# Own PSUM tiles for a weight product, spread copies and a re-cut last tile in a fused attention and maxout kernel

**Chip, cores, metric.** One core of one Trainium2 chip. The metric is the device time of one execution in microseconds, the median of several runs. All ratios are of fast runs: a run over 1.5% above the fastest of its kernel counts as slow and is left out.

## The reference

Block attention with a Sinkhorn-normalised block permutation, then a maxout MLP without bias. Cut to what matters here:

```python
# q, k, v: (4, 8, 768, 64); sort_net: (4, 8, 8, 8)
P = sinkhorn(sort_net, 5 rounds)
k_sorted, v_sorted = P applied to the 8 blocks of k and v
attn = softmax(q_b @ k_sb.T / 8) @ v_sb            # per block of 96
x = attn_out as (3072, 512)
h1, h2 = x @ w1, x @ w2                            # (3072, 1024)
return np.maximum(h1, h2) @ w_out                  # (3072, 512), float32
```

The kernel uses max(h1, h2) = relu(h1 - h2) + h2, so out = relu(x (W1 - W2)) Wout + x (W2 Wout). It computes W2 Wout (512 x 512, "wc") once: 32 transposes of W2, then four groups of eight matmuls. That work stands in the first of four batches, between its attention and its output products.

## The kernel before

All PSUM tiles come from one pool of four buffers of two banks each. TensorE's program is hand-ordered: `units` are the MLP steps of a batch, and attention steps of the next batch are put between them. The parts concerned (cuts marked with `# ...`):

```python
psum = ctx.enter_context(tc.tile_pool(name="psum", bufs=4, space=bass.MemoryType.PSUM))

def w2_transposes(t, eng):          # half t of W2: 16 transposes into one tile
    ps = ps_bf16("tw_ps")
    for n in range(16):
        # ... nc.tensor.matmul(ps[:, n*128:(n+1)*128], w2_sb[...], ident, is_transpose=True)
    def out():
        w = 2048 // len(eng)
        for n, e in enumerate(eng):  # "AD": first half on ScalarE, second on VectorE
            evac(w2T[...][:, n*w:(n+1)*w], ps[:, n*w:(n+1)*w], w, two_x=True, eng=e)
    return out

def w_product(dmt, eng=None):        # two products share a tile, one copy for both
    m = dmt % 2
    if m == 0:
        wc_ps[0] = ps_f32("wc_ps")
    for fb in range(NFB):
        nc.tensor.matmul(wc_ps[0][:, m*512:(m+1)*512], w2T[:, fb, ...], wo_sb[:, fb, :], ...)
    if m == 1:
        evac(wc[:, dmt-1:dmt+1, :]..., wc_ps[0], 1024, eng=eng)
# ...
# batch 0: v of the later batches is turned by 8 copies of 12 columns on VectorE
VA[1:6] = [(lambda f=f, g=g: (f(), g())) for f, g in zip(VA[1:6], tns)]
TR[0:2] = [(lambda f=f, g=g: (f(), g())) for f, g in zip(TR[0:2], tns[5:])]
SC[7:] = [lambda f=SC[7], g=tns[7]: (f(), g())]
# ...
steps[-1:] = group(VA[1], TR[0])     # a values step and an x transpose stand in one step
```

SC, VA and TR are scores, values and x-transpose steps. The last output tile of 128 tokens is cut by columns into pieces, each with its own PSUM tile, copy and store: `(0, 256, "A"), (256, 384, "D"), (384, 512, "A")`.

The softmax here doesn't subtract the row's maximum and nothing guards it: scores larger than these inputs give would overflow.

Of the kernel before, what the change touches and what calls it, by code (L numbers as in the profile page):

```python
# [15 lines left out]
def kernel(  # L16
# [16 lines left out]
    nc = tc.nc  # L33
# [4 lines left out]
    B, H, S, D = q.shape  # L38
# [26 lines left out]
    def ps_f32(name):  # L65
        return psum.tile([128, 1024], FP32, tag="ps", name=name)

    def ps_bf16(name):
        return psum.tile([128, 2048], BF16, tag="ps", name=name)
# [21 lines left out]
    def pick(a_ns, d_ns):  # L91
        if load["A"] + a_ns <= load["D"] + d_ns:
            load["A"] += a_ns
            return "A"
        load["D"] += d_ns
        return "D"

    def evac(out_ap, in_ap, n, two_x=False, eng=None):
        a_ns, d_ns = (200 + n) / 1.2, (130 + (n / 2 if two_x else n)) / 0.96
        if eng:  # L100
            load[eng] += a_ns if eng == "A" else d_ns
        if (eng or pick(a_ns, d_ns)) == "A":
            nc.scalar.copy(out=out_ap, in_=in_ap)  # L103
        else:
            nc.vector.tensor_copy(out=out_ap, in_=in_ap)  # L105
# [16 lines left out]
    for n in range(NE):  # L122
        t = big.tile([BLK, 8 * BLK + 32], BF16, tag=f"e{n}", name=f"e{n}")
# [35 lines left out]
    w2_sb = big.tile([128, HP, DFF], BF16, tag="w2", name="w2_sb")  # L159
# [16 lines left out]
    ident = const.tile([128, 128], BF16, tag="ident", name="ident")  # L176
# [345 lines left out]
    w2T = big.tile([128, NFB, DMODEL], BF16, tag="w2T", name="w2T")  # L522
    wc = big.tile([128, HP, DMODEL], BF16, tag="wc", name="wc")

    def w2_transposes(t, eng):
        ps = ps_bf16("tw_ps")
        for n in range(16):
            fb, dmt = t * 4 + n // 4, n % 4
            nc.tensor.matmul(  # L529
                ps[:, n * 128 : (n + 1) * 128],  # L530
                w2_sb[:, dmt, fb * 128 : (fb + 1) * 128],
                ident,
                is_transpose=True,
                start=True,
                stop=True,
            )
        def out():
            w = 2048 // len(eng)
            for n, e in enumerate(eng):
                evac(  # L540
                    w2T[:, t * 4 : t * 4 + 4, :].rearrange("p f d -> p (f d)")[
                        :, n * w : (n + 1) * w
                    ],
                    ps[:, n * w : (n + 1) * w],
                    w,
                    two_x=True,
                    eng=e,
                )

        return out  # L550

    wc_ps = {}

    def w_product(dmt, eng=None):
        m = dmt % 2
        if m == 0:
            wc_ps[0] = ps_f32("wc_ps")
        for fb in range(NFB):
            nc.tensor.matmul(  # L559
                wc_ps[0][:, m * 512 : (m + 1) * 512],  # L560
                w2T[:, fb, dmt * 128 : (dmt + 1) * 128],
                wo_sb[:, fb, :],
                start=(fb == 0),
                stop=(fb == NFB - 1),
            )
        if m == 1:
            evac(wc[:, dmt - 1 : dmt + 1, :].rearrange("p t n -> p (t n)"), wc_ps[0], 1024, eng=eng)


    g_tiles = {}  # L570
# [33 lines left out]
    def out_products(dst, b, ti, n0=0, n1=512, part=None):  # L604
        ch, off = divmod(ti * 128, TCH)
        for m in range(NFB + HP) if part is None else range(part * 6, part * 6 + 6):
            hp = m - NFB
            nc.tensor.matmul(  # L608
                dst,
                g_tiles[b, ch, m // 2][:, m % 2, off : off + 128]  # L610
                if m < NFB
                else xT[:, b % 2, ch, hp % 2, hp // 2, off : off + 128],
                wo_sb[:, m, n0:n1] if m < NFB else wc[:, hp, n0:n1],
                start=(m == 0),
                stop=(m == NFB + HP - 1),
            )
# [16 lines left out]
    def moe_out_last(ti, pieces):  # L633

        tok0 = (B - 1) * S + ti * 128
        for n0, n1, eng in pieces:
            ps = ps_f32("out_ps")
            out_products(ps[:, 0 : n1 - n0], B - 1, ti, n0, n1)
            o = opool.tile([128, n1 - n0], FP32, tag=f"o{ti}{n0}", name="o", bufs=1)
            if eng == "A":  # L640
                nc.scalar.copy(out=o, in_=ps[:, 0 : n1 - n0])
            else:
                nc.vector.tensor_copy(out=o, in_=ps[:, 0 : n1 - n0])
            (nc.scalar if eng == "A" else nc.sync).dma_start(
                out=out[tok0 : tok0 + 128, n0:n1], in_=o
            )
# [28 lines left out]
    SC, VA, TR = att(0)  # L675
# [37 lines left out]
    def load_rest():  # L713
# [5 lines left out]
        2: [SC[6], SC[7], VA[5]],  # L719
        3: [  # L720
            VA[6],
            VA[7],
            lambda: w2_transposes(1, "AD")(),
            lambda: x_transposes(0, 2, "A"),
            lambda: [turn(second, c) for c in (0, 12, 24)],
        ],
# [22 lines left out]
    for b in range(B):  # L749
        units = [lambda t=t: moe_h(b, 0, t, None if b else "A") for t in range(4)]  # L750
        if b == 0:
            units[0] = lambda: None
            units[1] = lambda: None
        wps = [lambda dmt=dmt: w_product(dmt, "A" if dmt == 1 else None) for dmt in range(4)]
        if b == 0:
            units += wps[:2]
        units += [lambda t=t: moe_h(b, 1, t) for t in range(4)]
        cost = [1.3] * 8
        if b == 0:
            units += wps[2:]  # L760
            cost[4:4] = [1.7] * 2
            cost += [1.7] * 2
        units += [
            lambda ti=ti, part=part: moe_out(b, ti, part)
            for ti in range(6 if b < B - 1 else 4)
            for part in range(2)
        ]
        cost += [1.3] * 12
        if b == B - 1:
            units += [  # L770
                lambda: moe_out_last(4, [(0, 512, "D")]),
                lambda: moe_out_last(5, [(0, 256, "A"), (256, 384, "D"), (384, 512, "A")]),
            ]
        steps, lo = [], 2
        load["A"] = load["D"] = 0.0
        if b < B - 1:
            qs = [lambda half=half: q_transposes(1, half) for half in range(2)]
            if b < 2:
                tail[18 - 4 * b] = [lambda two=two: pair_q(b + 2, two) for two in range(2)]
                tail[18 - 4 * b] += [lambda half=half: q_transposes(b + 2, half) for half in range(2)]  # L780
            ks = [lambda t=t, b=b: sort_k(b + 1, t) for t in range(3)]
            SC, VA, TR = att(b + 1)

            def group(*fs):
                return [lambda: [f() for f in fs]]

            if b == 0:
                lo = 10
                tail[9][2:2] = ks
                vs = [lambda t=t: sort_v(1, t) for t in range(4)]  # L790
                tns = [lambda c=c: turn(both, c) for c in range(0, BLK, 12)]
                VA[1:6] = [(lambda f=f, g=g: (f(), g())) for f, g in zip(VA[1:6], tns)]
                TR[0:2] = [(lambda f=f, g=g: (f(), g())) for f, g in zip(TR[0:2], tns[5:])]
                SC[7:] = [lambda f=SC[7], g=tns[7]: (f(), g())]
                steps = group(*vs[:3]) + qs[:1] + group(*SC[0:2], vs[3]) + qs[1:] + VA[:1]
                steps += group(*SC[2:5]) + VA[1:2]
            elif b == 1:
                vs = [lambda t=t: sort_v_pair(2, t) for t in range(8)]
                steps = group(*ks) + group(*vs[:2]) + group(*SC[0:2], late_loads)
                steps += group(*vs[2:4]) + group(*vs[4:6]) + group(*vs[6:]) + group(*SC[2:4]) + VA[:2]  # L800
            else:
                steps = group(*ks) + group(*SC[0:2])
                steps += VA[:1] + group(*SC[2:5]) + VA[1:2]
            rest = SC[4:] if b == 1 else SC[5:]
            steps[-1:] = group(VA[1], TR[0])
            steps += VA[2:3] + group(VA[3], TR[1])
            steps += group(*rest[:-1]) + VA[4:5] + rest[-1:] + group(VA[5], TR[2])
            steps += VA[6:7] + group(VA[7], TR[3])
        done = 0
        for n, unit in enumerate(units):  # L810
            unit()
            for step in tail.get(n, []):
                step()
            total = sum(cost[lo:-2])
            want = -(-len(steps) * sum(cost[lo : n + 1]) // total)
            while done < min(want, len(steps)):
                steps[done]()
                done += 1
        tail = {}
# [28 lines left out]
```

## Time and profile before

| | before |
|---|---|
| median, first three runs | 171.54 us (171.15 to 171.66) |
| span in the profile | 169.6 us |
| TensorE / VectorE / ScalarE busy | 96 / 54 / 47% |
| start of the last ScalarE copy to the end of the span | 3.5 us |

TensorE is the bound, so a change pays where TensorE's stream has a hole or where the end gets shorter.

### The profile page before, as it was taken

To read this page: it belongs to the slowest core of one execution; us is meant where nothing else is said; L and a number is where in the kernel's file an instruction comes from. 1 tells how busy PE (TensorE), PEld (TensorE's weight loads), DVE (VectorE), ACT (ScalarE), POOL (GpSimd) and SP (SyncE) were. 2 spreads that over 40 slices of the span, in tenths; PEclk is the share of its full clock that TensorE was granted. 3 is DMA by queue.
4 is the path that set the end of the run, shared out by engine and by line. 5 is a ranking of instruction groups with operands and counts; after the bars stand their busy time and mean duration, and the time that the engine had idled before them with its cause. 6 is when DMAs were issued, how large, how long until landed. Compare 5 with 4: busy or idle time off the path is not lost.

```text
span 169.6 us, 4551 instructions
## 1 busy us (share of the span) xinstructions
PE 162.3 (96%) x2015; PEld 97.0 (57%) x2015; DVE 91.8 (54%) x198; ACT 80.4 (47%) x98; POOL 25.3 (15%) x40
## 2 busy tenths in 40 slices
PE   7799999999999999999999999999999999999991
PEld 7638766736666554457665545566554546654461
DVE  4979677689245399847674448074552422330040
ACT  3598975756855554046774350446505404312000
POOL 7944372243300000000510000000000000000000
PEclk9999999999999999999999999999999999999999
DMA  3999999999999652994199349930025173000342
GB/s 47 201 206 207 199 207 206 209 202 206 215 220 198 106 170 52 140 238 151 10 199 169 92 126 215 194 120 6 0 50 150 34 203 128 0 0 0 124 157 94
DMA packets 29811, 23.11 MB, mean 136 GB/s; under 512 B 16672, under 2 KB 24736, under 8 KB 29792
## 3 DMA queue, kind: packets, MB, share of 16 engines
q0 software_dynamic: 10304, 12.58, 43.7%
q1 hardware_dynamic: 19200, 10.04, 23.9%
q8 instruction: 16, 0.26, 0.6%
q10 hardware_dynamic: 288, 0.20, 0.4%
q14 instruction: 3, 0.02, 0.0%
HBM read 25.17 MB, written 6.29 MB: 186 GB/s over the span
## 4 chain that ended last, share of the span: by engine, by line
PE 87%; DVE 6%; ACT 3%; DMA 1%; issue 1%
PE out_ps L608 37%; PE h_ps L581 26%; PE o_ps L471 5%; PE k_ps L377 4%; PE s_ps L444 4%; PE wc_ps L559 3%; PE v_ps L398 2%; PE v_ps L419 1%; PE tw_ps L529 1%; PE tq_ps L347 1%; DMA p_sb<-in_sort_net_dram 1%; PE tq_ps L352 1%; DVE colsum L226 1%; PE o_ps L81 1%; PE tx_ps L509 1%
## 5 line engine op out<-in xcount | busy, mean ns | idle before, releaser
L608 PE MATMUL out_ps<-wo_sb,g 128*128 128x512 bf16 (+2 forms) x208 | 48.3, 363 | 0.0
L581 PE MATMUL h_ps<-xT,w_sb 128*128 128x384 bf16 x256 | 44.8, 326 | 0.2 <-ACT g L595 0.2
L581 PEld LDWEIGHTS <-w_sb 128*128 128x128 bf16 x256 | 24.0, 98 | 15.7 <-issue 0.2
L452 ACT ACTIVATE e<-s_ps 96x768 bf16<-96x768 f32 x32 | 24.2, 804 | 16.1 <-PE s_ps L444 15.9
L608 PEld LDWEIGHTS <-g 128*128 128x128 bf16 x208 | 17.5, 97 | 15.3
L595 ACT ACTIVATE g<-h_ps 128x768 bf16<-128x768 f32 x21 | 16.9, 810 | 18.0 <-PE h_ps L581 18.0
L608 PE MATMUL out_ps<-wc,xT 128*128 128x512 bf16 (+2 forms) x104 | 25.0, 362 | 0.0
L103 ACT COPY o<-out_ps 128x1024 f32<-128x1024 f32 x9 | 9.1, 1012 | 30.0 <-PE out_ps L608 25.7
L597 DVE TENSOR_SCALAR g<-h_ps 128x768 bf16<-128x768 f32 x11 | 10.5, 955 | 22.5 <-PE h_ps L581 22.5
L488 DVE TENSOR_TENSOR x<-o_ps,rs 96x512 bf16<-96x512 f32 x32 | 22.0, 687 | 1.1
L482 DVE RECIPROCAL rs<-o_ps 96x8 f32<-96x8 f32 x32 | 6.4, 199 | 20.5 <-PE o_ps L471 20.4
L608 PEld LDWEIGHTS <-xT 128*128 128x128 bf16 x104 | 9.9, 97 | 11.0
L209 DVE COPY v_dc<-v_raw 64x768 bf16<-64x768 bf16 (+2 forms) x18 | 15.4, 897 | 0.1
L471 PEld LDWEIGHTS <-e 96*128 96x128 bf16 x256 | 11.6, 97 | 6.7 <-DVE x L488 0.5
L471 PE MATMUL o_ps<-v_sb,e 96*128 96x65 bf16 x256 | 12.9, 193 | 0.1
L105 DVE CAST v_sb<-v_ps 96x1024 bf16<-96x1024 f32 x7 | 8.5, 1214 | 5.6 <-PE v_ps L398 5.2
L103 ACT CAST v_sb<-v_ps 96x1024 bf16<-96x1024 f32 x9 | 8.9, 1014 | 1.6 <-PE v_ps L419 1.0
L444 PEld LDWEIGHTS <-kT 64*128 64x128 bf16 x256 | 6.0, 94 | 5.4 <-issue 4.6
L444 PE MATMUL s_ps<-qT,kT 64*128 64x96 bf16 x256 | 8.6, 204 | 0.1
L103 ACT CAST kT<-k_ps 128x1024 bf16<-128x1024 f32 x8 | 7.7, 1021 | 1.1 <-PE k_ps L377 1.1
L105 DVE COPY o<-out_ps 128x1024 f32<-128x1024 f32 x2 | 2.4, 1224 | 10.6 <-PE out_ps L608 9.5
L81 PEld LDWEIGHTS <-fill 128*128 128x128 bf16 x109 | 6.9, 120 | 2.2 <-DVE fill L72 1.2
(76 smaller groups left out, 138.4 us busy)
## 6 DMA issues: line engine op xcount, KB each, us to landing
out_dram<-o SPq DMA_DIRECT2D x11, 512.0 KB, 3.1
k_raw<-in_k_dram POOLq DMA_DIRECT2D x12, 256.0 KB, 10.3
q_raw<-in_q_dram POOLq DMA_DIRECT2D x4, 768.0 KB, 12.6
v_raw<-in_v_dram POOLq DMA_DIRECT2D x6, 384.0 KB, 13.8
w_sb<-in_moe_w_dram POOLq DMA_DIRECT2D x3, 512.0 KB, 15.9
wo_sb<-in_moe_w_out_dram POOLq DMA_DIRECT2D x2, 512.0 KB, 18.8
v_raw<-in_v_dram POOLq DMA_DIRECT2D x3, 256.0 KB, 4.9
w_sb<-in_moe_w_dram POOLq DMA_DIRECT2D x2, 256.0 KB, 14.1
```

What stands on the lines that cost most here:

```text
L81: nc.tensor.matmul(ps[:, 0:w], w0, fill[:, 0:w], start=True, stop=True)
L103: nc.scalar.copy(out=out_ap, in_=in_ap)
L105: nc.vector.tensor_copy(out=out_ap, in_=in_ap)
L209: nc.vector.tensor_copy(out=dst, in_=src)
L444: nc.tensor.matmul(ps[:, h2 * 512 + ii * 128 : h2 * 512 + ii * 128 + BLK], kT[b][rows, (hp * 8 + i) * BLK : (hp * 8 + i) * BLK + 128], rhs ...
L452: nc.scalar.activation(out=e[:, 0 : 8 * BLK].rearrange("p (t c r) -> p t c r", t=8, r=R), in_=ps[0:BLK].rearrange("p (t f) -> p t f", t=8) ...
L471: nc.tensor.matmul(ps[:, h2 * 512 + ii * 65 : h2 * 512 + (ii + 1) * 65], e[:, (h2 * 4 + ii) * BLK : (h2 * 4 + ii) * BLK + 128], v_sb[:, m0 ...
L488: nc.vector.tensor_tensor(out=x, in0=ov[:, :, :, 0:D], in1=rs.to_broadcast([BLK, 2, 4, D]), op=ALU.mult,)
L581: nc.tensor.matmul(h_ps[t][:, m * 512 : m * 512 + TCH], w1_sb[:, hp, fb * 128 : (fb + 1) * 128], xT[:, b % 2, ch, hp % 2, hp // 2, :], sta ...
L595: nc.scalar.activation(out=g, in_=src, func=AF.Relu)
L597: nc.vector.tensor_scalar(out=g, in0=src, scalar1=0.0, scalar2=None, op0=ALU.max)
L608: nc.tensor.matmul(dst, g_tiles[b, ch, m // 2][:, m % 2, off : off + 128] if m < NFB else xT[:, b % 2, ch, hp % 2, hp // 2, off : off + 12 ...
```

## The change

Its intent: give each W2-Wout product its own PSUM tile, so that no buffer is held over the work between two products; let both engines empty the W2 transposes at once; never put two v copies into one step; and cut the last output tile so that a small piece remains for the end. The core of the diff:

```diff
 def w2_transposes(t, eng):
-    ps = ps_bf16("tw_ps")
-    for n in range(16): ...
+    w = 16 // len(eng)
+    for p, e in enumerate(eng):
+        ps = ps_bf16("tw_ps")
+        for n in range(w): ...
+        outs.append((ps, p, e))          # one tile, one copy for each engine
 def w_product(dmt, eng=None):
-    m = dmt % 2
-    if m == 0:
-        wc_ps[0] = ps_f32("wc_ps")
+    ps = ps_f32("wc_ps")
     ... eight matmuls ...
-    if m == 1:
-        evac(wc[:, dmt - 1 : dmt + 1, :]..., wc_ps[0], 1024, eng=eng)
+    evac(wc[:, dmt, :], ps[:, 0:512], 512, eng=eng)
@@ steps of batch 0
             VA[6],
+            lambda: w2_transposes(1, "AD")(),
             VA[7],
-            lambda: w2_transposes(1, "AD")(),
@@ last tile
-  moe_out_last(5, [(0, 256, "A"), (256, 384, "D"), (384, 512, "A")])
+  moe_out_last(5, [(0, 384, "D"), (384, 512, "A")])
@@ turns of v
-  VA[1:6] = ...; TR[0:2] = ...; SC[7:] = ...
+  for step, n in [((VA, 0), 0), ((VA, 1), 1), ((VA, 2), 2), ((VA, 4), 3),
+                  ((TR, 1), 4), ((VA, 5), 5), ((SC, 7), 6), ((VA, 6), 7)]:
+      step[0][step[1]] = lambda f=step[0][step[1]], g=tns[n]: (f(), g())
```

Part 1 is the transposes, part 2 the products, part 3 the turns, part 4 the last tile.

More of the change, by code (lines that the diff above doesn't have):

```diff
@@ L525, in w2_transposes @@
     def w2_transposes(t, eng):
-        ps = ps_bf16("tw_ps")
-        for n in range(16):
-            fb, dmt = t * 4 + n // 4, n % 4
-            nc.tensor.matmul(
-                ps[:, n * 128 : (n + 1) * 128],
-                w2_sb[:, dmt, fb * 128 : (fb + 1) * 128],
-                ident,
-                is_transpose=True,
-                start=True,
-                stop=True,
-            )
+        w = 16 // len(eng)
+        outs = []
+        for p, e in enumerate(eng):
+            ps = ps_bf16("tw_ps")
+            for n in range(w):
+                fb, dmt = t * 4 + (p * w + n) // 4, n % 4
+                nc.tensor.matmul(
+                    ps[:, n * 128 : (n + 1) * 128],
+                    w2_sb[:, dmt, fb * 128 : (fb + 1) * 128],
+                    ident,
+                    is_transpose=True,
+                    start=True,
+                    stop=True,
+                )
+            outs.append((ps, p, e))
         def out():
-            w = 2048 // len(eng)
-            for n, e in enumerate(eng):
+            for ps, p, e in outs:
+                fb = t * 4 + p * w // 4
                 evac(
-                    w2T[:, t * 4 : t * 4 + 4, :].rearrange("p f d -> p (f d)")[
-                        :, n * w : (n + 1) * w
-                    ],
-                    ps[:, n * w : (n + 1) * w],
-                    w,
+                    w2T[:, fb : fb + w // 4, :].rearrange("p f d -> p (f d)"),
+                    ps[:, 0 : w * 128],
+                    w * 128,
                     two_x=True,
@@ L550, in w2_transposes @@
         return out
-    wc_ps = {}
     def w_product(dmt, eng=None):
-        m = dmt % 2
-        if m == 0:
-            wc_ps[0] = ps_f32("wc_ps")
+        ps = ps_f32("wc_ps")
         for fb in range(NFB):
             nc.tensor.matmul(
-                wc_ps[0][:, m * 512 : (m + 1) * 512],
+                ps[:, 0:512],
                 w2T[:, fb, dmt * 128 : (dmt + 1) * 128],
@@ L565, in w_product @@
             )
-        if m == 1:
-            evac(wc[:, dmt - 1 : dmt + 1, :].rearrange("p t n -> p (t n)"), wc_ps[0], 1024, eng=eng)
+        evac(wc[:, dmt, :], ps[:, 0:512], 512, eng=eng)
     g_tiles = {}
@@ L771 @@
                 lambda: moe_out_last(4, [(0, 512, "D")]),
-                lambda: moe_out_last(5, [(0, 256, "A"), (256, 384, "D"), (384, 512, "A")]),
+                lambda: moe_out_last(5, [(0, 384, "D"), (384, 512, "A")]),
             ]
@@ L791 @@
                 tns = [lambda c=c: turn(both, c) for c in range(0, BLK, 12)]
-                VA[1:6] = [(lambda f=f, g=g: (f(), g())) for f, g in zip(VA[1:6], tns)]
-                TR[0:2] = [(lambda f=f, g=g: (f(), g())) for f, g in zip(TR[0:2], tns[5:])]
-                SC[7:] = [lambda f=SC[7], g=tns[7]: (f(), g())]
+                for step, n in [((VA, 0), 0), ((VA, 1), 1), ((VA, 2), 2), ((VA, 4), 3), ((TR, 1), 4), ((VA, 5), 5), ((SC, 7), 6), ((VA, 6), 7)]:
+                    step[0][step[1]] = lambda f=step[0][step[1]], g=tns[n]: (f(), g())
                 steps = group(*vs[:3]) + qs[:1] + group(*SC[0:2], vs[3]) + qs[1:] + VA[:1]
```

## The prediction

> **What bounds the kernel now.** I read the page's busy times and slices first, then the chain that ended last in order of time, then the timeline of single engines around the places that the diff touches, then the waits and the DMA issues.
>
> ```profile
> span 169.6 us, 4551 instructions
> PE 162.3 (96%) x2015; PEld 97.0 (57%) x2015; DVE 91.8 (54%) x198; ACT 80.4 (47%) x98; POOL 25.3 (15%) x40
> ...
> PE   7799999999999999999999999999999999999991
> ...
> DVE  4979677689245399847674448074552422330040
> ACT  3598975756855554046774350446505404312000
> ```
>
> TensorE (PE) is busy 96% of the span and in every slice between head and tail; VectorE (DVE) and ScalarE (ACT) are half idle. A change can therefore only save time where PE has a hole, or in the head and the tail. What could be had at most is 169.6 - 162.3 = 7.3 us, most of it head (PE's first two slices are 7, before 12.6 us the chain is the Sinkhorn loop on DVE) and tail (PE ends at 166.05, the span at 169.6: 3.5 us), which the diff hardly touches. The holes that it does touch are in the chain, where it leaves PE:
>
> ```profile
> 32.69 0.91 PE tw_ps L529 x16
> 33.60 0.02 issue
> 33.62 1.02 ACT w2T L103
> 34.64 0.02 issue
> 34.66 0.70 DVE w2T L105
> 35.37 0.05 issue
> 35.41 0.60 PE wc_ps L559 x2
> ...
> 47.60 1.02 ACT v_sb L103
> 48.62 0.04 issue
> 48.66 0.83 PE tq_ps L347 x12
> ...
> 51.25 1.02 ACT wc L103
> 52.27 0.04 issue
> 52.32 0.83 PE tq_ps L347 x12
> ```
>
> Columns: start, length, engine and tile. The chain detours three times over copies out of PSUM. But a detour is not a loss of its whole length, for PE has other work meanwhile. The timeline of the engines shows the loss:
>
> ```profile
> 34.66 0.69 DVE L105 COPY w2T<-tw_ps 128x1024 bf16<-128x1024 bf16 x1 [0.42 <-ACT w2T L103]
> 48.66 0.83 PE L347 MATMUL tq_ps<-ident,q_pair 128*128 128x128 bf16 x12 [0.16 <-ACT v_sb L103]
> 52.32 0.83 PE L347 MATMUL tq_ps<-ident,q_pair 128*128 128x128 bf16 x12 [0.19 <-ACT wc L103]
> 59.16 1.56 DVE L209 COPY v_dc<-v_raw 128x768 bf16<-128x768 bf16 x2
> 166.07 0.27 ACT L641 COPY o<-out_ps 128x128 f32<-128x128 f32 x1 [0.97 <-PE out_ps L608]
> 166.36 0.51 ACTq L644 DMA_DIRECT2D out_dram<-o  x1
> ```
>
> The first line: the second half of the W2 transposes was copied only after ACT was through with the first half, since both halves are one tile. The next two: PE sat idle 0.16 and 0.19 us before the q transposes, for a PSUM buffer. The fourth: two turns of v back to back on DVE. The last two: how the kernel ends.
>
> **What the Trainium skill says.** "PSUM — Partial Sum Buffer", section "PSUM bank collisions raise a hardware error": accesses of two engines have to be kept apart by bank, and in different banks they run side by side. A half of 1024 bf16 is 2 KiB a partition, one bank by that page's table; so ACT before DVE is owed to the tile, not to the hardware, and two tiles can drain together. The trace of before has only the serial order (0.42 us of wait). "TensorE: Matmul & The Clock Gate", section "Back-to-back issue gap": N/2.4 + 2.5 ns a matmul when warm. The trace agrees: twelve products of 512 columns start 2.59 us apart (150.27, 152.86, 155.45), 0.216 each; eight of 384 columns take 1.30 us in the chain, 0.1625 each; the pieces of 256 and 128 columns start 163.22, 164.53, 165.20, so 0.109 and 0.056 each. "ScalarE: Activation LUTs", section "What ACT_TABLE_LOAD costs": 186 ns + 0.833 ns an element with immediate scale and bias. The trace is some 27 ns under that: 265, 372 and 1012 ns for 128, 256 and 1024 columns, so a 512-column copy is about 265 + 384 x 0.834 = 585 ns.
>
> **Part 1, two tiles for the second W2 transposes, moved ahead of the last values step.** What it can win: the first W2-Wout product group starts at 33.76 and runs four of eight matmuls on the half that has been there since 27.7; by the 0.216 spacing the fifth could start at 34.63 and starts at 34.69, the seventh could start 35.12 and starts 35.41. Loss 0.06 + 0.29 = 0.35 us, the ceiling. What it adds: four PSUM buffers go round in the order in which they are released (inferred: at 48.66 the q transposes waited for the v_sb copy just before, not for the held wc tile). With one more tile, the order is values 6, tw A, tw B, values 7, x transposes, wc 0; so wc 0 takes the buffer of tw A and waits for its copy. PE: values 6 at 32.04; eight transposes (0.45) to about 32.75; tw B to 33.2; values 7 (0.25) and x transposes (0.34) to 33.8. ACT: the relu of 32.24 to 33.05 is ahead of the copy of A; then 1.01 us to about 34.03. The product group, ready at about 33.8, so starts at 34.03 and its eight matmuls run without a break for 1.73 us, to 35.76. Before, the x transposes behind them started at 35.85. **Net gain 0.09 us** of the 0.35: the wait for w2T becomes a wait for a buffer. DVE copies B at about 33.43 to 34.12 (before 34.66 to 35.35) and hands on the last values step at 35.07, in time for all who read it.
>
> **Part 2, W2-Wout products in own tiles.** A pair held a buffer from the first product to the copy after the second, with v sorting and q transposes between; so three buffers were left. That is what made the two q-transpose waits. With a tile each: the first q transposes take wc 2's buffer (its copy: products end at 46.99, ACT free at 47.1, 0.585 us, done 47.7, needed 48.5: no wait); wc 3 takes v 0's (ACT, done 48.7, needed 49.3); the two scores take v 1's and v 2's; the second q transposes take wc 3's (products end 51.1, copied by 51.7, needed 52.0: no wait). I replayed the kernel's own balance of ACT against DVE by its formulas: all four 512-column copies fall to ACT; of the three v copies the second goes to DVE and the third to ACT, the other way round than now; both end before 49.6, for scores at 51.0. Cost: four copies of 585 against two of 1012 ns, 0.32 us more on ACT, which idles half the time here. **Gain 0.16 + 0.16 = 0.32 us** (PE could not have started the second at once, hence not 0.19).
>
> **Part 3, turns one to a step.** The eight turns of 0.82 us stay. Now steps after the second and the fourth values step have two; then one each, and the first moves from 59.16 to about 55.7, where DVE is idle. Its data: the last v load is issued at 42.56 with 12.5 us to landing, so there at 55.06 at the latest. Between 58.3 and 71 DVE lags up to 1 us behind PE, but the chain there is PE's pieces end to end (1.30, 0.24, 1.30, ...; 1.40 after scores). **0.0 us.**
>
> **Part 4, the last tile.** PE: 256 + 128 + 128 columns take 12 x (0.109 + 0.056 + 0.056) = 2.65 us; 384 + 128 take 12 x (0.1625 + 0.056) = 2.62. **Gain 0.03 us.** The last copy and DMA (128 columns, ACT) are the same; the 384-column copy on DVE, 0.56 us by interpolation of 292 and 692 ns, ends near 165.9 and its DMA is issued 0.4 us before the last. One DMA fewer is in flight; I count nothing for it.
>
> Sum: 0.09 + 0.32 + 0 + 0.03 = 0.44 us. From 171.54: **171.1 us**.
>
> **Rivals.** First, the middle comes out cleaner: if the relu does not hold up the copy of tw A, or wc 0 gets another buffer than I infer, part 1 gives its full 0.35 and the time is 170.85. For it: ACT's relu ends at 33.05, only 0.3 us after A is written. Against it: the copy alone needs 1.01 us and only 0.6 us of other PE work lies behind B. Second, a new wait eats it: more tiles through four buffers put each allocation behind a copy of an engine that may be late. An ACT wait of 0.2 us at two places would leave 171.5. For it: ACT is full from 44.3 to 49.5. Against: each margin worked out above is 0.3 us or more. Third, the tail: the 384-column DMA may land last. Issued at 165.96 it would have to take over 2.7 us; the issues of before took 2.3 to 3.9, and the skill ("DMA: Bandwidth & Descriptors", section "Anatomy of one DMA — SWDGE (gpsimd) path") puts most of the fixed cost in the receipt of the write, not in the bytes; the trace agrees in kind (512 KB 2.8 us, 256 KB 3.9, 64 KB 2.3 and 2.8). If it lands at 3.9 the end moves by up to +1.2 and the kernel is at 172.0; I give that little weight, as the 256 KB one of before landed at 168.04, ahead of the last. Fourth, a turn moved ahead of its data would stall DVE; but the next DVE work is at 58.3, so that stays hidden.
>
> **Range and chances.** The best case is 0.35 + 0.32 + 0.03 = 0.7 us, so 170.8; the runs of before spread over 0.5 us. I take 170.7 to 171.5. A gain of 2% would be 3.4 us, five times the best case, and a loss of 2% has no source here: 0.98 for within 2%, 0.01 for each side.
>
> **What would show it.** Right: in the chain no copy of w2T by DVE after ACT, no v_sb or wc copy ahead of the q transposes, and no idle there; the two w2T copies overlap; a wait of 0.2 us of the first product group for ACT's w2T copy; four wc copies near 585 ns, all on ACT; PE's last matmul 0.4 us earlier; the same 3.5 us after it. Wrong: PE idle anew ahead of v sorting, scores or the first output, a span that ends on the 384-column DMA, or PE ending early without the time following.

## More of the kernel before

```profile
q8 instruction: 16, 0.26, 0.6%
```

Sixteen packets of 16 KB each (0.26 MB): blocks of instructions fetched while the kernel runs.

## The result, and the profile after

| | before | after |
|---|---|---|
| median | 171.41 us (171.05 to 171.66, 6 runs) | 170.13 us (169.97 to 170.18, 6 runs) |
| ratio | | 0.9927 (0.9913 to 0.9940) |
| span in the profile | 169.57 | 168.28 |
| last ScalarE copy starts | 166.07 | 165.28 |
| from there to the end of the span | 3.50 | 3.00 |

A ratio is the mean time of one kernel's fast runs over that of the other's of the same rounds, so not quite the ratio of the medians. The gain is 1.3 us where 0.44 was predicted: within 2%, as forecast, but outside the range of 170.7 to 171.5. The table already splits it: 0.79 us before the last copy, 0.50 us after it.

The page after: the span, the busy times and the instruction queue.

```profile
span 168.3 us, 4525 instructions
...
PE 162.1 (96%) x2003; PEld 96.7 (57%) x2003; DVE 92.2 (55%) x198; ACT 80.2 (48%) x99; POOL 25.0 (15%) x40
...
q8 instruction: 15, 0.25, 0.6%
```

One instruction fetch fewer. The chain of after in order of time (start, length, engine and tile), for the places that the prediction showed of before:

```profile
32.46 0.90 PE tw_ps L533 x16
33.36 0.24 PE o_ps L471 x8
33.60 0.39 PE tx_ps L509 x8
34.00 0.02 issue
34.02 1.89 PE wc_ps L559 x8
...
48.39 0.78 PE tq_ps L347 x12
49.16 1.73 PE wc_ps L559 x8
...
51.80 0.78 PE tq_ps L347 x12
```

In this stretch no copy stands in the chain any more; it stays on TensorE. The first product group runs its eight matmuls in one piece from 34.02 on. The q transposes take 0.78 us where they took 0.83, and start at 48.39 for 48.66 and at 51.80 for 52.32.

A place that the prediction had passed over as having no holes: two scores groups (x16) a little later. First the chain of before, then of after.

```profile
61.36 0.60 PE s_ps L444 x16
```

```profile
60.76 0.45 PE s_ps L444 x16
```

The same 16 matmuls take 0.15 us less. The gap between the two kernels goes from 0.60 to 0.76 us right here. VectorE's timeline, before and after, shows why:

```profile
59.16 1.56 DVE L209 COPY v_dc<-v_raw 128x768 bf16<-128x768 bf16 x2
60.64 0.20 DVE L482 RECIPROCAL rs<-o_ps 96x8 f32<-96x8 f32 x1
60.88 0.69 DVE L488 TENSOR_TENSOR x<-o_ps,rs 96x512 bf16<-96x512 f32 x1
```

```profile
58.56 0.82 DVE L209 COPY v_dc<-v_raw 128x768 bf16<-128x768 bf16 x1
59.30 0.20 DVE L482 RECIPROCAL rs<-o_ps 96x8 f32<-96x8 f32 x1
59.53 0.69 DVE L488 TENSOR_TENSOR x<-o_ps,rs 96x512 bf16<-96x512 f32 x1
```

Before, two turns in a row put off the x product of the third values step to 61.57. By the order in which buffers are released, the second of the two scores groups takes the PSUM tile that this product reads. The single records agree: the first group starts at 61.29, the second only at 61.62, 0.05 us after that product. After, the product is done at 60.22, ahead of both groups (60.69 and 60.87).

The end. First before, then after: the DMA issues of the last two tiles, with size and us from issue to landing.

```profile
out_dram<-o SPq DMA_DIRECT2D x1, 256.0 KB, 3.9
...
out_dram<-o ACTq DMA_DIRECT2D x1, 128.0 KB, 3.2
...
out_dram<-o SPq DMA_DIRECT2D x1, 64.0 KB, 2.8
out_dram<-o ACTq DMA_DIRECT2D x1, 64.0 KB, 2.3
```

```profile
out_dram<-o SPq DMA_DIRECT2D x1, 256.0 KB, 2.0
out_dram<-o SPq DMA_DIRECT2D x1, 192.0 KB, 1.9
out_dram<-o ACTq DMA_DIRECT2D x1, 64.0 KB, 1.7
```

The store of 256 KB belongs to the tile before the last, which the diff doesn't touch, and still lands in 2.0 us for 3.9. So something other than the cut of the last tile is at work. The trace's packet records name a candidate. The instruction queue's last packet of before (16,384 bytes) started at 165.01 us and took 1.49 us on one of the DMA engines, just when the last stores were on their way. After has no such packet later than 141.6.

### The profile page after: what moved, and what is told of

It is laid out like the page before. It is cut to its first block, busy times and chain, and to the rows that moved or that the text cites. A ratio compares the mean times of both kernels' runs of the same rounds, so it can differ in the third digit from the quotient of the medians.

```text
span 168.3 us, 4525 instructions
## 1 busy us (share of the span) xinstructions
PE 162.1 (96%) x2003; PEld 96.7 (57%) x2003; DVE 92.2 (55%) x198; ACT 80.2 (48%) x99; POOL 25.0 (15%) x40
## 4 chain that ended last, share of the span: by engine, by line
PE 90%; DVE 6%; DMA 1%; ACT 1%; issue 1%
PE out_ps L607 38%; PE h_ps L580 26%; PE o_ps L471 5%; PE wc_ps L559 4%; PE k_ps L377 4%; PE s_ps L444 4%; PE v_ps L398 2%; PE v_ps L419 1%; PE tw_ps L533 1%; DMA p_sb<-in_sort_net_dram 1%; PE tx_ps L509 1%; PE tq_ps L352 1%; PE tq_ps L347 1%; DVE colsum L226 1%; PE o_ps L81 1%
## 5 line engine op out<-in xcount | busy, mean ns | idle before, releaser
L607 PEld LDWEIGHTS <-g 128*128 128x128 bf16 x200 | 17.0, 97 | 15.7
L209 DVE COPY v_dc<-v_raw 64x768 bf16<-64x768 bf16 (+2 forms) x18 | 15.6, 898 | 0.4 <-DMA v_raw<-in_v_dram 0.3
```

Of the source, the lines that this page charges most:

```text
L209: nc.vector.tensor_copy(out=dst, in_=src)
L607: nc.tensor.matmul(dst, g_tiles[b, ch, m // 2][:, m % 2, off : off + 128] if m < NFB else xT[:, b % 2, ch, hp % 2, hp // 2, off : off + 12 ...
```

## The experiments

The theory to test: **(a)** the missing instruction fetch shortens the end. The rival: **(b)** the number or order of the output stores does. For the rest, the parts alone. "Head to end" below is the time from the first W2 transposes (25.56 us in before) to the last ScalarE copy, so that a head of 0.1 us more or less drops out; it measures TensorE's stream. "End" is from that copy's start to the end of the span. These come from the chains and spans; the fetch columns come from the packet records:

```
kernel             PE instr  head to end   end   fetches  last fetch         last 2048-byte store packet ends
before               4032      140.51      3.50    16     165.01 to 166.50   167.52
after                4008      139.70      3.00    15     140.60 to 141.62   165.05
p1_only              4032      140.39      3.91    16     165.16 to 166.93   167.95
p2_only_b            4032      140.02      3.72    16     164.56 to 166.14   167.15
p3_only              4032      140.35      3.62    16     164.91 to 166.48   167.48
p4_only              4008      140.49      3.00    15     141.20 to 142.53   165.85
before_fewer_pe_b    4008      140.53      2.82    15     143.67 to 144.68   165.84
after_plus12         4032      139.70      3.35    16     162.42 to 164.26   166.58
after_plus6          4020      139.70      2.99    16     170.20 to 171.66   165.17
fewer_none           4008      140.51      2.80    15     143.55 to 144.47   165.58
fewer_p3             4008      140.35      2.81    15     143.72 to 144.67   165.62
fewer_p1             4008      140.39      2.80    15     143.57 to 144.71   165.70
```

Kernels whose stream is the same agree in head to end within some 0.02 us: 140.49 to 140.53 for before, p4_only, before_fewer_pe_b and fewer_none, 139.70 for all three of after.

**p2_only**, part 2 alone (the diff's `w_product` and nothing else).

> Only the W2-Wout products in own PSUM tiles. By the prediction's figures: 0.32 us saved (two waits of 0.16). By the start-to-start reading of the two traces: the two waits for a buffer cost 0.23 and 0.27 us of PE's stream, so 0.50 us saved (ratio about 0.997). The end of the kernel, from the last ACT copy's start to the end of the span (3.5 us in before, 3.0 after), is to stay at 3.5, and the 16th instruction fetch to stay, since PE's instructions stay 4032.

171.12 us median of fast runs, before 171.33, ratio 0.9982 (0.9962 to 1.0002). The profiled execution took 912 us: its TensorE ran the last 96 output matmuls in 95 us (15.6 in before), while ScalarE's and VectorE's instructions kept their length (806 ns for 804 for the exponentials). The clock of 1.0 that the result lists for it is no reading: the trace holds no clock record. It is left out as slow, and why it was slow is not known. So the run was made again.

> W2-Wout products in own tiles alone, once more for the same reason. Start-to-start reading: the first output products start at 52.6 to 52.7 for 53.15 before (0.50 us saved; the prediction said 0.32), PE ends 0.5 us earlier, the end stretch stays 3.5 us with 16 fetches.

170.96 against 171.33, ratio 0.9976 (0.9961 to 0.9992). Head to end is 0.49 us shorter, the end is not, the fetches are 16. The two buffer waits were worth 0.49 us, not 0.32.

**p3_only**, part 3 alone (the diff's loop over `tns`).

> Only the turns one to a step. By the prediction: 0.0 us. Rival, read from the two traces: before, two turns back to back held up the x product of the values step whose PSUM buffer the later of two scores groups needs, and those 16 scores matmuls took 0.67 us where they now take 0.52; so 0.15 us saved. End of the kernel unchanged at 3.5 us.

171.52 against 171.33, ratio 1.0004 (0.9983 to 1.0026): unclear by the time. The trace has the 0.16 us in head to end, and the scores group at 0.45 us:

```profile
61.35 0.45 PE s_ps L444 x16
```

**p4_only**, part 4 alone (the diff's last line).

> Only the last output tile in pieces of 384 and 128 columns. By the prediction: 0.03 us. By what the traces show: 0.5 to 0.55 us, nearly all of it after PE has ended (3.5 us from the start of the last ACT copy to the end becomes 3.0). Two theories give that: (a) 24 PE instructions fewer (4008 for 4032), so that the 16th fetch of a 16 KB block of instructions, which in before held one of the 16 DMA engines for 1.49 us from 165.0 us on, isn't made; (b) one output DMA fewer in flight, or none ahead of the last on ACT's queue. (a) expects 15 instruction fetches on the page.

170.86 against 171.33, ratio 0.9966 (0.9946 to 0.9985), 15 fetches. Head to end gains 0.02 us, no more than such traces differ by; the end gains 0.50. Both theories had said so.

**before_fewer_pe**, which tells them apart: the kernel before, its three last pieces untouched.

```diff
-keep_streaming(ps_f32("fill_ps"), 18 * 512, width=96)    # 96 warm-up matmuls (of zeros, never read) at the head
+keep_streaming(ps_f32("fill_ps"), 18 * 512, width=110)   # 84
```

> The kernel before with the same columns of warm-up matmuls at the head in 84 pieces in place of 96, so 24 PE instructions fewer, as many as the new last tile saves; its output pieces stay three. Theory (a), the instruction fetch: 15 fetches, the last stretch 3.0 us for 3.5, 0.5 us saved. Theory (b), the number or order of output DMAs: nothing saved, 3.5 us.

170.79 (fast runs) against 171.33, ratio 0.9971 (0.9951 to 0.9991), and again a profiled execution of the far slower kind (568 us). Repeated:

> The kernel before with 24 PE instructions fewer at the head, run once more, because the profiled execution of the first run was one of a slow state[...] and shows nothing of the end. Theory (a), the instruction fetch: PE's end as in before (last ACT copy at about 166.1, so that the head is not what moved), 3.0 us from there to the end for 3.5, three output DMAs of the last tile all the same. Theory (b), the number of output DMAs: 3.5 us, and the saving of the first run must show as an earlier end of PE.

170.71 (170.65 to 170.84) against 171.33, ratio 0.9961 (0.9945 to 0.9976). The last copy starts at 166.09 (166.07 in before), so nothing ahead of it moved. Its DMA issues of the last two tiles:

```profile
out_dram<-o SPq DMA_DIRECT2D x1, 256.0 KB, 2.0
out_dram<-o ACTq DMA_DIRECT2D x1, 128.0 KB, 1.7
out_dram<-o SPq DMA_DIRECT2D x1, 64.0 KB, 1.6
out_dram<-o ACTq DMA_DIRECT2D x1, 64.0 KB, 1.6
```

The same four stores as before, each 0.7 to 1.9 us faster; the end is 2.82 us for 3.50. Theory (b) falls. Twelve warm-up matmuls fewer at the head, 150 us away, save what the re-cut tile saves and a little more, because there are 24 instructions fewer and so one fetch fewer.

The table shows one thing more. Without a late fetch the end takes 2.80 to 2.82 us with the three old pieces and 2.99 to 3.00 with the two new ones (p4_only, after, after_plus6). So the new cut itself makes the end about 0.2 us longer, and the 0.50 us are some 0.7 for the fetch less this 0.2. By that estimate, after with its old last tile and 12 warm-up matmuls fewer would be some 0.2 us faster than after; it was not run, and the times of p4_only and before_fewer_pe_b are too close to show the 0.2.

**p1_only**, part 1 alone (the diff's `w2_transposes` and the order of the list).

> Only the second W2 transposes in two tiles and ahead of the last values step. The prediction said 0.09 us saved, the trace of after shows 0.11 us (the x transposes behind the first product group start at 35.74 for 35.85), with a wait of about 0.2 us of the first product for the copy of the first tile. So 0.1 us. Rival, a clean middle: 0.35 us.

171.47 against 171.53, ratio 0.9988 (0.9972 to 1.0004). Head to end 0.12 us shorter, as expected; not the clean middle of 0.35.

**after_more_pe**, the kernel after with `width=86` at the head (108 warm-up matmuls).

> The kernel after with the warm-up matmuls in 108 pieces in place of 96, same columns, so that PE has 4032 instructions again as before had; output pieces as in after. Theory (a), the instruction fetch: 16 fetches, one near the end holding a DMA engine, and up to 0.5 us of the gain lost (170.4 to 170.7 where after had 170.1). Theory (b): nothing lost, 170.1.

170.63 (170.40 to 170.74): it looks like a hit for (a), and is none. Its trace has 16 fetches, but the last lies at 162.97 to 164.45. The stores beside it were slower (512 KB in 3.7 us for 2.8, 256 KB in 3.2 for 2.0), but the last two landed in 1.9 and 1.7 us as in after, and the end takes 2.99 us. What it lost is at the start: its chain goes through the landing of the first q load at 16.75 us, and TensorE's work came 0.54 us late. Its time tells nothing of the end; hence the next two, which add matmuls in the warm part instead.

**after_plus12** and **after_plus6**.

```diff
-keep_streaming(ps, n)                 # warm-up inside sort_k, sort_v (plus6),
+keep_streaming(ps, n, width=256)      # and in values and the first h products (plus12)
```

> after_more_pe moved the head as well (PE's work started 0.54 us late in its trace), so its time tells nothing of the end. This is the kernel after with 12 more warm-up matmuls where PE is warm and the columns stay the same (pieces of 256 for 512 columns), so 4032 PE instructions. Theory (a): 16 fetches; the fetch may end before the last output's packets, as in after_more_pe (it ended 3.0 us before the last packet), and then costs nothing: 170.1 to 170.3; if it is on while the last packets come, up to 0.5 us more. Theory (b): 170.1.

> As after_plus12 with 6 more matmuls, 4020 PE instructions: the fetch, if there is a 16th, comes 12 instructions later in the stream and so nearer to the end. Theory (a): either 15 fetches and 170.1, or 16 with the last of them within 3 us of the last packet and up to 0.5 us lost (170.3 to 170.7). Theory (b): 170.1.

plus12: 170.26 (170.08 to 170.50), 16 fetches, the last from 162.42 to 164.26 for 1.85 us; the end takes 3.35 us. plus6: 170.92 (170.57 to 171.44), 16 fetches, but the last starts at 170.20, after the span of 168.4 us is over. The span is as in after and the time is 0.8 us longer, so the loss lies outside the span; presumably the execution is not over before the fetch has landed, but no run here separates that. Its stores land in 2.0, 1.9 and 1.7 us, as in after: with 16 fetches too, they are slow only beside one. So the cost of a late fetch depends on where it falls: 0.7 to 1.1 us on top of the last stores (ends of 3.50 to 3.91 with the old pieces, for 2.80 to 2.82), 0.35 in the trace shortly before them (plus12; its time, 170.26, is within (a)'s 170.1 to 170.3 for a fetch that costs nothing), 0.8 after them, and nothing at the end of after_more_pe. The expectation of plus6 was a miss: no such late fetch was foreseen, and 170.92 lies above its 170.3 to 170.7.

**fewer_none, fewer_p3, fewer_p1**: parts 3 and 1 on a base without the late fetch, for the times of before spread up to 1.1 us (170.87 to 172.01), those of kernels without that fetch mostly 0.2 to 0.4 (after_reordered, below, 0.7).

> The kernel before with 24 PE instructions fewer at the head, as the quiet base for the next two on the same chip: 170.7 us, spread under 0.3.

> That base and the turns one to a step: 0.16 us less than the base if the hold-up of the scores by the double turn is real, 0.0 by the prediction.

> That base and the W2 transposes in two tiles, ahead of the last values step: 0.1 us less than the base (prediction 0.09, trace 0.11); a clean middle would give 0.35.

170.73 (170.46 to 170.80), 170.51 (170.32 to 170.69) and 170.58 (170.54 to 170.76) us, five runs each. Part 3 shows as 0.2 us of the medians, part 1 as 0.15 (0.05 of the means); with 0.2 to 0.4 us of spread and five runs neither is proven by the times, though part 1 is not the 0.35 of a clean middle. The traces repeat both: head to end is 0.16 and 0.12 us shorter than in fewer_none, as it was in p3_only and p1_only against before.

**after_reordered** and **after_reordered_b**, attempts at a better version. In after, the first product waits until 34.02 for the PSUM buffer of the first transposed half. Its buffer becomes an earlier one if the last values step goes behind it:

```diff
     lambda: w2_transposes(1, "AD")(),
-    VA[7],
     lambda: x_transposes(0, 2, "A"),
-    lambda: [turn(second, c) for c in (0, 12, 24)],            # only in _b
...
-4: [lambda: x_transposes(0, 3, "A"), load_rest, ...],
+4: [VA[7], load_rest, ...],                                    # in _b with the turns behind VA[7]
-5: [lambda: block_diagonals(1), ...],
+5: [lambda: x_transposes(0, 3, "A"), lambda: block_diagonals(1), ...],
```

> An attempt at a version that beats both: in the kernel after, the last values step goes behind the first W2-Wout product and its x transposes behind the second, so that the first product takes the PSUM buffer of values step 6 (free at 33.5) and no longer waits for ScalarE's copy of the first half of W2 (done 33.97). Saves up to 0.2 us; but the last x transposes come late (37.3), and the h products that read them may wait 0.1 us. So 0.0 to 0.1 us better than after, 170.0 to 170.1.

> after_reordered did away with the first product's wait (it started at 33.5 for 34.0), but put the three turns of v, which wait for a v load until 34.9, ahead of the last values step on DVE, so that PE waited 0.8 us for that step's x. Here the turns stand behind that step. Expected: first product at 33.5, the last values step's x done by about 36.2, no PE wait for it, so 0.1 to 0.25 us better than after, 169.9 to 170.05. If the later turns or the later x transposes hold up the h products, 170.1 or more.

170.91 (170.59 to 171.32) and 170.48 us: both slower than after, and both misses, for at most 170.1 was hoped for. From the first W2 transposes to the last copy they take 1.25 and 0.40 us longer than after. The wait did go (the product starts at 33.5), and TensorE waited later instead. First the timeline of after_reordered, then of after_reordered_b:

```profile
38.19 0.51 PE L509 MATMUL tx_ps<-ident,x 96*128 96x96 bf16 x8 [0.84 <-DVE x L488]
```

```profile
38.76 5.04 PE L580 MATMUL h_ps<-xT,w_sb 128*128 128x384 bf16 x30 [0.47 <-ACT xT L103]
```

The first waited for x behind turns whose v load landed late; the second for the copy of the late x transposes, behind a wc copy on ScalarE. So after stays the best version tried.

## Why the prediction was wrong

Head to end and end in one sum, each term as the run of its part shows it: 0.12 + 0.49 + 0.16 + 0.02 = 0.79 us in TensorE's stream (after against before: 0.81), and 0.50 us at the end. Predicted were 0.09 + 0.32 + 0.0 + 0.03 = 0.44, and 0 at the end.

- **Part 1, right.** 0.12 for 0.09. The mechanism held in detail: ScalarE's copy of the first half at 32.96 to 33.97, VectorE's at 33.40 to 34.09 beside it, the product group at 34.02 (predicted 34.03), waiting for a buffer and no longer for the data. That two engines can empty two tiles in different banks at once, as the prediction took from the skill's PSUM page, the trace of after agrees with: 0.57 us of overlap.
- **Part 2, right in mechanism, too small.** 0.49 for 0.32. The mis-sized term is "0.16 + 0.16", taken from the idle time between matmul records. A matmul that doesn't wait starts before the record of the one ahead of it ends (48 v matmuls have 190 ns each and start 30 ns apart), and behind a wait the stream also restarts with only one weight load done: the twelve q transposes took 0.83 us in the chain for 0.78. Start to start, a wait cost about 0.25 us. The predicted replay of the buffers and of the balance of the two engines was right: four wc copies of 0.59 us, all on ScalarE, no new wait.
- **Part 3, wrong.** "The chain there is PE's pieces end to end ... 0.0 us." The chain was end to end because the wait lay inside a merged piece: 0.60 us for 16 scores matmuls, where other such pieces of 16 have 0.45 to 0.47 (and one of 0.52 comes after an idle stretch). p3_only removes it. The prediction had seen VectorE lag 1 us behind and had not asked whose PSUM buffer comes free late by it.
- **Part 4, TensorE right, the end wrong.** TensorE gained 0.02 for the predicted 0.03, both too small to tell from nothing. The spacings behind the 0.03 are right: the section that the prediction names ("TensorE: Matmul & The Clock Gate", "Back-to-back issue gap") gives N/2.4 + 2.5 ns for a single matmul alone, and 81 and 131 ns for 128 and 512 columns in a stream of weight loads and matmuls; the streams here have 56 and 216, which is the formula. The failing step is "the last copy and DMA ... are the same" and "one DMA fewer is in flight; I count nothing for it": not the store itself, but a fetch of instructions beside it, decided by the program's length. before_fewer_pe_b shows the cause with all stores unchanged. The prediction's third rival, a slower end, has the sign of the new cut itself (0.2 us, not up to 1.2); the missing fetch hides it. The hint was in the profile: 256 KB landing in 3.9 us, where 512 KB took 2.8, was put down to the cost of a write receipt.
- **The range** was built on 0.7 us as the best case, from the terms that had been seen. It left no room for terms that had not, and two of the four parts had such. Two sums of the rivals slip, without touching the range: 171.54 less 0.7 is 170.84, and 171.1 and 1.2 are 172.3, not 172.0.

Not settled: why 4008 instructions take 15 fetches and 4020 take 16, how late a fetch comes relative to the instruction that triggers it (with 4032 instructions the last one fell at 165.0 in before and at 162.4 and 163.0 in the two variants of after), and the time outside the span in after_plus6.

## What to carry to other kernels

Size a wait of TensorE from start to start against the same stream without a wait, and look for pieces of the chain that are longer than their like: the idle column shows too little, and nothing where pieces are merged. When VectorE or ScalarE lags, ask which buffer it frees late. And look at the instruction queue in the list of DMA queues: in a long unrolled kernel a dozen instructions more or less, anywhere, can decide whether a fetch falls on the last stores; a few runs with other program lengths cost little and, here, were worth 0.4%. Compare a new cut of the last stores only between kernels whose last fetch falls alike.

## What the Trainium skill lacked or had wrong

- "Runtime: NRT & Kernel Launch", section "Instruction fetch mechanics", says that an engine's instructions are refilled in blocks of 16 KiB, 256 instructions, by a DMA queue of the sequencer, and that crossing a block costs one DMA tail-bump, "mostly hidden". The block size agrees (packets of 16,384 bytes). The count does not follow from matmuls and weight loads alone: 16 for 4032 and 4020, 15 for 4008. What is lacking: the fetch takes DMA time beside the kernel's own transfers. Here one packet took 1.49 us, and the stores in flight landed in 2.3 to 3.9 us where they take 1.6 to 2.0 without it; the end was 0.7 us longer.
- "DMA: Bandwidth & Descriptors", section "Anatomy of one DMA — SWDGE (gpsimd) path": its fixed 2 us, mostly receipt, is near the 1.6 to 2.0 us of undisturbed stores of 64 to 256 KB here (which SyncE and ScalarE issue, not GpSimd). The 3.9 us that the prediction put down to it fell to 2.0 without the late instruction fetch; the page has no word on that cause.
- "Perfetto Trace Analysis", section "Summary: the profiler window per engine type", says that a TensorE record ends at an estimated end. What is lacking is the consequence: the idle time between two records understates a wait, here 0.16 us for about 0.25.
- No page has slow executions of the size seen twice: 567 and 910 us spans of kernels that otherwise take 169, with the last 96 output matmuls in 59 and 95 us for 15.6, VectorE's and ScalarE's instructions of the usual length, and no clock record in the trace. No cause was found.
